# A seven-product second layer from group 1 on, and a planner that places batch 1's units

## The chip, the cores and the metric

The kernel runs on one core of a Trainium2 chip. A core has TensorE (PE) for matrix products, VectorE (DVE), ScalarE (ACT) and GpSimd (POOL) for elementwise work, and SyncE (SP), which here only issues DMAs. Each engine works through its own list of instructions in order, and semaphores tie the lists together. The metric is the time of one execution on the device in microseconds (us), as the median of several runs.

## The reference

The input x holds 8 batches of 3008 tokens with 256 channels. Each batch goes through a real Fourier transform along its tokens, is multiplied by a complex filter (1505 frequencies by 256 channels), and is transformed back. The result goes, token by token, through a feed-forward layer with a squared ReLU:

```python
X = np.fft.rfft(x, axis=1)
y = np.fft.irfft(X * (filt_r + 1j * filt_i)[None], n=3008, axis=1)
y = y.reshape(24064, 256)
h = np.maximum(y @ w_in, 0.0)          # w_in: 256 x 2048
out = (h * h) @ w_out                  # w_out: 2048 x 256
```

## The kernel before

**Feed-forward.** The 24064 tokens are cut into NG = 47 groups of 512, and each group into SLOTS = 8 slots. The main loop runs over all slots s, with g = s // 8 and k = s % 8. In a slot, `ffn_g1` computes an eighth of the first layer for group g (L553: four matmuls of 512 columns into psH, then the ReLU on ACT, L557); `ffn_sq` squares two slots' worth on DVE (L564). The second layer of a group runs one group later and takes one of two forms:

- the plain form, `ffn_g2` and `ffn_out`: eight matmuls of 256 columns a slot, 64 a group (L573), and two copies of psO by ACT (L584) before the stores;
- the seven-product form, for the groups in `SEVEN`: the product is split into a 2 x 2 block form, so that 7 block products of 16 matmuls with 128 columns each, 112 a group (L666), replace eight. `sums` makes four sums of the squared activations on DVE (L639, L642, L645, L648); `products` runs the matmuls one slot later than the plain form would, empties psX and psY by four copies on ACT and three additions on DVE (L681, L687), and stores in its sixth and seventh slot. `make_t` prepares four differences of the second layer's weights on DVE, once, in four slots.

In the kernel before, `SEVEN` is groups 6 to 45; groups 0 to 5 and 46 take the plain form. In the slot in which one form hands over to the other, no second-layer product runs.

**Fourier transform.** It is done by matmuls in small units, which run between the feed-forward's instructions. For batch b, 16 `unit_a` (L358) transform along one factor of the length and write u, which goes to DRAM (dU) and comes back turned round (`read_u`, ut). Then 12 `unit_b` (L442) each give a psB tile, from which DVE makes the product with the filter (L450); two DMAs on POOL's queue (L457) add its two halves. 12 `unit_p` (L487) do the first inverse step from that product; ACT copies psP to ze, and SP writes it to DRAM (dZ). `read_z` brings it back as zt, and 16 `unit_y` (L523) give the y that the feed-forward reads. Odd `unit_y` are copied out by DVE (L532), others by ACT (L530). `load_x` (L195, on POOL's queue) brings in the next batches. All four kinds of unit take their PSUM tile from one pool, psF, of two buffers.

**Order of work.** `fft_plan` writes a list of half slots. In a slot, the units of its first half come after `ffn_g1`, those of its second half after the second layer's products. Units in `fixed` go to the half slot that their formula gives, even where another is there already. Units in `units` are placed by a rule: each kind in turn, in the order `unit_b`, `unit_p`, `unit_y`, `unit_a`; each takes the free half slot nearest to its formula's, with a penalty where more than two of the four neighbours are taken. `moves` holds the DMAs, which may share a half slot. Batch 1's `unit_b` and `unit_p` are in `fixed`; those of later batches are in `units`. Batch 0 is transformed in a prologue before slot 0. A unit is written below as B1.4: `unit_b` number 4 of batch 1; A, P and Y likewise.

Of the kernel before, what the change touches and what calls it, by code (L numbers as in the profile page):

```python
# [20 lines left out]
SLOTS = 8  # L21
# [89 lines left out]
def kernel(  # L111
# [16 lines left out]
    NG = T // TG  # L128
# [408 lines left out]
    def ffn_g1(g, s):  # L537
        if s == 0:
            h2s[g] = p_h2.tile([128, NJT, TG], F16, tag="h2", name=f"h2_{g}")
        h2 = h2s[g]  # L540
        ps = psH(f"psH_{g}_{s}")
        segs = []
        t = g * TG
        while t < (g + 1) * TG:
            b, r = divmod(t, S)
            n = min((g + 1) * TG - t, S - r)
            segs.append((t - g * TG, b, r, n))
            t += n
        for i in range(2):
            jt = 2 * s + i  # L550
            for o, b, r, n in segs:
                for dt in range(2):
                    nc.tensor.matmul(ps[:, i, o:o + n],  # L553
                                     sWin[:, dt, jt * 128:(jt + 1) * 128],
                                     yts[b][:, dt, r:r + n],
                                     start=(dt == 0), stop=(dt == 1))
        nc.scalar.activation(out=h2[:, 2 * s:2 * s + 2, :], in_=ps, func=AF.Relu)  # L557
# [18 lines left out]
    def ffn_out(g, s):  # L576

        step = 1 if g == NG - 1 else 2
        if (s + 1) % (2 * step):
            return  # L580
        n = s // 2 + 1 - step
        ost = p_out.tile([128, 2, 256], F32, tag="ost", name=f"ost_{g}_{s}")
        h0 = n % 2
        nc.scalar.copy(out=ost[:, h0:h0 + step, :], in_=pso[g][:, h0:h0 + step, :])  # L584
        store(g, n, step, ost)
# [25 lines left out]
    def make_t(k):  # L611

        w = sWout.rearrange("p (q e) c -> p q e c", e=2)
        b11, b12 = w[:, :, 0, 0:128], w[:, :, 0, 128:256]
        b21, b22 = w[:, :, 1, 0:128], w[:, :, 1, 128:256]
        if k == 0:
            sg["t"] = p_t.tile([128, 4, 8, 128], F16, tag="t", name="sT")
        t = sg["t"]
        i0, i1 = ((b12, b11), (b22, t[:, 0]), (b22, b12), (b21, t[:, 1]))[k]
        nc.vector.tensor_sub(out=t[:, k], in0=i0, in1=i1)  # L620
        sg["w"] = {1: b11, 2: b21, 3: b22, 4: t[:, 3], 5: t[:, 0], 6: t[:, 1], 7: t[:, 2]}
# [33 lines left out]
    def products(g, k):  # L655

        f = sg[g]
        for p, m0, m1 in PARTS[k]:
            if p == 1 and m0 == 0:
                f["x"] = psO(f"psX_{g}").rearrange("p a (t c) -> p a t c", t=2)  # L660
            if p == 2 and m0 == 0:
                f["y"] = psO(f"psY_{g}").rearrange("p a (t c) -> p a t c", t=2)
            o = f["x"][:, 0] if p in (1, 6, 7, 4) else f["y"][:, 0 if p == 2 else 1]
            for m in range(m0, m1):
                q, t = divmod(m, 2)
                nc.tensor.matmul(o[:, t, :], f[p][:, q, 128 * t:128 * t + 128], sg["w"][p][:, q, :],  # L666
                                 start=(m == 0 and p in (1, 2)), stop=(q == 7),
                                 skip_group_check=True)
            if m1 < 16:
                continue  # L670
            if p == 1:
                f["top"] = p_out.tile([128, 2, 256], F32, tag="ost", name=f"top_{g}")
                nc.scalar.copy(out=f["top"][:, :, 0:128], in_=o)
            elif p == 6:
                nc.scalar.copy(out=f["top"][:, :, 128:256], in_=o)
            elif p == 7:
                f["bot"] = p_out.tile([128, 2, 256], F32, tag="ost", name=f"bot_{g}")
                nc.scalar.copy(out=f["bot"][:, :, 128:256], in_=o)
            elif p == 2:
                for v, i in ((f["top"][:, :, 0:128], 0), (f["bot"][:, :, 128:256], 1)):  # L680
                    nc.vector.tensor_add(out=v, in0=f["y"][:, i], in1=v)  # L681
            elif p == 4:
                nc.scalar.copy(out=f["bot"][:, :, 0:128], in_=o)
                store(g, 2, 2, f["bot"])
            elif p == 3:
                v = f["top"][:, :, 128:256]
                nc.vector.tensor_add(out=v, in0=o, in1=v)  # L687
                store(g, 0, 2, f["top"])
# [3 lines left out]
    def fft_plan():  # L692

        fixed, units, moves = [], [], []
        for b in range(1, B):
            f = (b * S // TG) * SLOTS - (48 if b > 1 else 40)
            d = 0
            if b == 1:
                for n in range(4, 16):
                    fixed.append(((n if n < 8 else n + 2 if n < 12 else 2 * n - 7) + n % 2 / 2,  # L700
                                  unit_y, 0, n))
                moves.append((7.5, read_z, 0, 3))
                for k in range(4):
                    moves.append(((4.5, 5.5, 7.5, 7.5)[k], cast_wout, k, nc.vector))
                for a in range(12, 16):
                    fixed.append((2 + a / 2, unit_a, b, a))
                moves.append((10.5, read_u, b))
                d = 7
            else:
                for a in range(16):  # L710
                    if a % 2 == 0 and b > 2:
                        moves.append((f + ((-57 + 2.3 * a) if b == 3 else (-66 + 2.75 * a)),
                                      load_x, b, a // 2))
                    units.append((f + (-16 + a, -46 + 2.1 * a, -56 + 2.75 * a)[min(b, 4) - 2],
                                  unit_a, b, a))
                moves.append((f + (2 if b == 2 else -6.5), read_u, b))
            for p in range(12):
                r = 14 + 15 * p / 11 if b == 1 else 6 + 28 * p / 11 if b == 2 else -2 + 36 * p / 11
                (fixed if b == 1 else units).append((f + r, unit_b, b, p))
                if b == 1 and 2 <= p < 10:  # L720
                    moves.append((f + r, load_x, 2, p - 2))
                (fixed if b == 1 else units).append((f + r + (4.5 if b == 1 else 7 - 2.5 * p / 11), unit_p, b, p))
            for c in range(4):
                moves.append((f + (40 + d / 7, 43, 48, 54)[c] - d, read_z, b, c))
            for n in range(16):
                (fixed if n < 4 else units).append((f + YN[n] - d, unit_y, b, n))
        work, used, done = {}, set(), {}
        for r, *u in fixed:
            h = int(2 * r)
            used.add(h)  # L730
            work.setdefault(h, []).append(u)
        rank = (unit_b, unit_p, unit_y, unit_a)
        for r, *u in sorted(units, key=lambda u: (rank.index(u[1]), u[0])):
            after = done.get((u[0], u[1]), -1)
            h = min((h for h in range(max(int(2 * r) - 3, after + 1), int(2 * r) + 12)
                     if h not in used),
                    key=lambda h: (sum(h + i in used for i in (-2, -1, 1, 2)) > 2) * 2
                    + abs(h - int(2 * r)))
            used.add(h)
            done[(u[0], u[1])] = h  # L740
            work.setdefault(h, []).append(u)
        for r, *u in moves:
            work.setdefault(int(2 * r), []).append(u)
        return work

    def run(plan, s, place):
        for f, *a in plan.get(2 * s + place, ()):
            f(*a)
# [10 lines left out]
    for k in range(2):  # L759
        c = slice(12 * k, 12 * k + 12)  # L760
# [26 lines left out]
    for k in range(6):  # L787
        if k % 3 == 0:
            sSPx.append(p_u.tile([128, 12, 128], F16, tag="u", name=f"sSPx_{k}"))
        c, o = slice(4 * k, 4 * k + 4), slice(4 * k % 12, 4 * k % 12 + 4)  # L790
# [26 lines left out]
    prologue[0] = False  # L817
    read_z(0, 2)

    SEVEN = range(6, NG - 1)  # L820
    work = fft_plan()

    for s in range((NG + 1) * SLOTS):
        g, k = divmod(s, SLOTS)
        if g < NG:
            ffn_g1(g, k)
        run(work, s, 0)
        if SEVEN[0] * SLOTS <= s < SEVEN[0] * SLOTS + 4:
            make_t(s % SLOTS)
        if (s - 1) // SLOTS - 1 in SEVEN:  # L830
            products((s - 1) // SLOTS - 1, (s - 1) % SLOTS)
        if g > 0 and g - 1 not in SEVEN:
            ffn_g2(g - 1, k)
        run(work, s, 1)
        if g > 0 and g - 1 not in SEVEN:
            ffn_out(g - 1, k)
        if g - 1 in SEVEN:
            sums(g - 1, k)
        if g < NG:
            ffn_sq(g, k)  # L840
# [30 lines left out]
```

## Time and profile before

| | before |
|---|---|
| median of 3 runs | 767.12 us (766.33 to 768.42) |
| the profiled execution's own time | 767.9 us |
| its span, first to last instruction | 766.1 us |
| PE busy | 751.9 us (98%) |
| DVE busy | 620.2 us (81%) |
| ACT busy | 579.2 us (76%) |
| POOL busy | 192.7 us (25%) |
| mean granted TensorE clock | 0.998 |

Busy times overlap: the engines work side by side. A matmul's end is modelled in the profile, and matmuls are pipelined, so that the time that one takes in a row of them is the distance between two starts and not the listed duration. Group 1 begins at 59.74 us, group 2 at 77.10, group 3 at 95.52, group 4 at 112.72, group 5 at 130.94, group 6 at 147.27 and group 7 at 163.82; each of these is the start of the group's first L553 matmul. Slot numbers count from slot 0, at 49.34 us.

### The profile page before, as it was taken

The numbers are of one execution on the slowest core, as the hardware profiler recorded it, in microseconds if no ns is written. First come the engines' busy times: TensorE is split into PE (matmuls) and PEld (weight loads), VectorE is DVE, ScalarE is ACT, GpSimd is POOL, SyncE is SP. The second block draws the span as 40 slices with busy tenths as digits, with TensorE's granted clock in tenths as the row PEclk, the third lists the DMA queues.
The fourth block names the chain that finished last, engine by engine and source line by source line (L and its number), as shares of the span: only waits on it lengthen the run. The fifth ranks groups of instructions, "written<-read, shape, count | busy, mean of one in ns | idle before, by whom it ended". The sixth has DMA issues, their size and how long they took to land.

```text
span 766.1 us, 19166 instructions
## 1 busy us (share of the span) xinstructions
PE 751.9 (98%) x8022; PEld 552.8 (72%) x8022; DVE 620.2 (81%) x679; ACT 579.2 (76%) x831; POOL 192.7 (25%) x260
## 2 busy tenths in 40 slices
PE   8989999999999999999999999999999999999998
PEld 6746666767777777877778777787777777777776
DVE  5856674579889888898979988798989989888783
ACT  3966777788878887788787877778876777777673
POOL 3800750133312331223212324043311222000000
PEclk9999999999999999999999999999999999999999
DMA  9985797756776457755575555765447334321011
GB/s 364 388 238 178 133 181 176 203 114 119 151 200 140 101 112 165 204 112 111 121 212 128 107 132 108 196 153 112 100 110 206 92 73 98 98 72 55 29 56 56
DMA packets 104943, 109.22 MB, mean 143 GB/s; under 512 B 9640, under 2 KB 93096, under 8 KB 102936
## 3 DMA queue, kind: packets, MB, share of 16 engines
q1 hardware_dynamic: 85704, 87.38, 36.8%
q0 software_dynamic: 19008, 20.43, 19.9%
q8 instruction: 63, 1.03, 0.6%
q14 instruction: 24, 0.20, 0.1%
q10 hardware_dynamic: 144, 0.18, 0.1%
HBM read 58.12 MB, written 48.23 MB: 139 GB/s over the span
## 4 chain that ended last, share of the span: by engine, by line
PE 87%; DVE 5%; DMA 5%; ACT 1%; issue 1%; SPq 0%; POOL 0%; DVEq 0%; ACTq 0%
PE psH L553 39%; PE psX L666 18%; PE psY L666 13%; PE psO L573 6%; PE psY L523 3%; PE psB L442 3%; PE psA L358 2%; DMA f<-in_filt_i_dram 2%; PE psP L487 2%; DVE prod L450 2%; DVE h L564 1%; DMA zt<-dZ 1%; DMA dZ<-ze 1%; PE psf L291 1%; DVE sum L645 1%
## 5 line engine op out<-in xcount | busy, mean ns | idle before, releaser
L557 ACT ACTIVATE h<-psH 128x1024 f16<-128x1024 f32 x376 | 385.0, 1025 | 153.3 <-PE psH L553 147.9
L553 PE MATMUL psH<-yt,sWin 128*128 128x512 f16 (+7 forms) x1728 | 388.5, 352 | 1.2 <-DVE yt L532 0.6
L564 DVE TENSOR_TENSOR h<-h 128x2048 f16<-128x2048 f16 (+1 forms) x192 | 229.9, 1198 | 55.2 <-ACT h L557 54.6
L457 POOL DMA_DIRECT2D prod<-prod x168 | 138.8, 970 | 440.1 <-DVE prod L450 432.8
L553 PEld LDWEIGHTS <-sWin 128*128 128x128 f16 x1728 | 152.8, 98 | 99.1 <-issue 5.0
L666 PEld LDWEIGHTS <-sum 128*128 128x128 f16 x2560 | 157.9, 98 | 18.4
L666 PEld LDWEIGHTS <-h 128*128 128x128 f16 x1920 | 118.9, 98 | 19.5
L450 DVE TENSOR_TENSOR prod<-psB,sF 128x1024 f16<-128x1024 f32 x84 | 102.5, 1220 | 25.2 <-PE psB L442 25.1
L666 PE MATMUL psX<-sT,sum 128*128 128x128 f16 x1280 | 91.0, 219 | 0.0
L666 PE MATMUL psY<-sT,sum 128*128 128x128 f16 x640 | 61.9, 219 | 0.0
L573 PE MATMUL psO<-sWout,h 128*128 128x256 f16 x448 | 56.9, 272 | 0.0
L532 DVE CAST yt<-psY 128x376 f16<-128x376 f32 x62 | 33.8, 545 | 27.5 <-PE psY L523 27.5
L362 ACT CAST u<-psA 96x512 f16<-96x512 f32 x90 | 52.1, 579 | 3.5 <-PE psA L358 3.1
L489 ACT CAST ze<-psP 128x512 f16<-128x512 f32 x84 | 49.0, 583 | 1.6 <-PE psP L487 1.6
L573 PEld LDWEIGHTS <-h 128*128 128x128 f16 x448 | 43.1, 98 | 9.1 <-issue 0.2
L642 DVE TENSOR_TENSOR sum<-sum,h 128x2048 f16<-128x2048 f16 x40 | 48.9, 1222 | 0.9
L666 PE MATMUL psY<-sWout,h 128*128 128x128 f16 x640 | 48.9, 219 | 0.0
L666 PE MATMUL psX<-sT,h 128*128 128x128 f16 x640 | 48.8, 219 | 0.0
L645 DVE TENSOR_TENSOR sum<-h 128x2048 f16<-128x2048 f16 x40 | 48.7, 1217 | 0.0
L648 DVE TENSOR_TENSOR sum<-h,sum 128x2048 f16<-128x2048 f16 x40 | 48.7, 1217 | 0.0
L666 PE MATMUL psY<-sWout,sum 128*128 128x128 f16 x640 | 48.6, 219 | 0.0
L639 DVE TENSOR_TENSOR sum<-h 128x2048 f16<-128x2048 f16 x40 | 48.6, 1216 | 0.0
(86 smaller groups left out, 684.4 us busy)
## 6 DMA issues: line engine op xcount, KB each, us to landing
zt<-dZ SPq DMA_DIRECT2D x64, 192.0 KB
dU<-u SPq DMA_DIRECT2D x28, 384.0 KB
prod<-prod POOLq DMA_DIRECT2D x168, 64.0 KB, 2.7
dZ<-ze SPq DMA_DIRECT2D x28, 384.0 KB
x<-in_x_dram POOLq DMA_DIRECT2D x40, 192.0 KB, 4.7
ut<-dU SPq DMA_DIRECT2D x7, 1024.0 KB
xw<-in_x_dram SPq DMA_DIRECT2D x6, 1024.0 KB
ut<-dU SPq DMA_DIRECT2D x7, 512.0 KB
```

The lines of the kernel that those rows point to most:

```text
L362: nc.scalar.copy(out=o, in_=pv)
L450: nc.vector.tensor_mul(out=prod, in0=ps.rearrange("p (a d) -> p a d", d=D).unsqueeze(1).to_broadcast([128, 2, 2, D]), in1=sF[:, :, 2 * p:2 ...
L457: nc.gpsimd.dma_start(out=prod[64 * i:64 * i + 64, 0], in_=prod[64 - 64 * i:128 - 64 * i, 1], accum_op=mybir.AluOpType.add)
L489: nc.scalar.copy(out=zes[(b, c)][:, 2 * i6:2 * i6 + 2, :], in_=ps.rearrange("p (a d) -> p a d", d=D))
L553: nc.tensor.matmul(ps[:, i, o:o + n], sWin[:, dt, jt * 128:(jt + 1) * 128], yts[b][:, dt, r:r + n], start=(dt == 0), stop=(dt == 1))
L557: nc.scalar.activation(out=h2[:, 2 * s:2 * s + 2, :], in_=ps, func=AF.Relu)
L564: nc.vector.tensor_mul(out=v, in0=v, in1=v)
L573: nc.tensor.matmul(pso[g][:, t % 2, :], h2s[g][:, jt, t * 128:(t + 1) * 128], sWout[:, jt, :], start=(jt == 0), stop=(jt == NJT - 1))
L642: nc.vector.tensor_sub(out=t, in0=f[5], in1=a11)
L645: nc.vector.tensor_sub(out=t, in0=a11, in1=a21)
L648: nc.vector.tensor_sub(out=t, in0=a12, in1=f[6])
L666: nc.tensor.matmul(o[:, t, :], f[p][:, q, 128 * t:128 * t + 128], sg["w"][p][:, q, :], start=(m == 0 and p in (1, 2)), stop=(q == 7), skip ...
```

## The change

The diff does three things.

- `SEVEN` starts at group 1 instead of group 6. `make_t` runs in slots 10 to 13 instead of 48 to 51. The slot without second-layer products is 16 instead of 56.
- Batch 1's `unit_b` and `unit_p` move from `fixed` to `units`, so that they are placed by the rule above, and their formula starts at 13.5 instead of 14. `load_x` of batch 2, which uses the same formula, moves by half a slot.
- The first `read_z` of batch 1 moves from half slot 34 to 33.5 (d is 7 for batch 1 and 0 for all others).

```diff
             for p in range(12):
-                r = 14 + 15 * p / 11 if b == 1 else 6 + 28 * p / 11 if b == 2 else -2 + 36 * p / 11
-                (fixed if b == 1 else units).append((f + r, unit_b, b, p))
+                r = 13.5 + 15 * p / 11 if b == 1 else 6 + 28 * p / 11 if b == 2 else -2 + 36 * p / 11
+                units.append((f + r, unit_b, b, p))
                 if b == 1 and 2 <= p < 10:
                     moves.append((f + r, load_x, 2, p - 2))
-                (fixed if b == 1 else units).append((f + r + (4.5 if b == 1 else 7 - 2.5 * p / 11), unit_p, b, p))
+                units.append((f + r + (4.5 if b == 1 else 7 - 2.5 * p / 11), unit_p, b, p))
             for c in range(4):
-                moves.append((f + (40 + d / 7, 43, 48, 54)[c] - d, read_z, b, c))
+                moves.append((f + (40 + d / 14, 43, 48, 54)[c] - d, read_z, b, c))
...
-    SEVEN = range(6, NG - 1)
+    SEVEN = range(1, NG - 1)
...
-        if SEVEN[0] * SLOTS <= s < SEVEN[0] * SLOTS + 4:
-            make_t(s % SLOTS)
+        if 10 <= s < 14:
+            make_t(s - 10)
```

## The prediction

> **What bounds the kernel now.** I read the busy times by group first. The stretches are cut at the first L553 matmul of groups 1 to 6, then a late group and the last whole one (us; busy us and instructions per engine; granted clock; DMA share; GB/s):
>
> ```profile
> 59.74:77.10 17.36, 16.91 (x124) 11.37 (x124) 10.71 (x14) 11.08 (x14) 0.59 (x2) 1.00 0.48 155
> 77.10:95.52 18.42, 17.45 (x136) 12.33 (x134) 11.37 (x10) 13.49 (x20) 13.79 (x19) 1.00 0.82 136
> 95.52:112.72 17.20, 17.20 (x122) 11.84 (x120) 11.75 (x11) 13.16 (x19) 10.93 (x15) 1.00 0.97 182
> 112.72:130.94 18.22, 17.31 (x127) 11.33 (x126) 8.79 (x10) 13.48 (x20) 1.01 (x2) 1.00 0.85 190
> 130.94:147.27 16.33, 16.14 (x158) 11.84 (x156) 8.19 (x9) 11.62 (x17) 0.79 (x2) 1.00 0.66 202
> 147.27:163.82 16.55, 16.55 (x128) 11.50 (x126) 11.71 (x14) 12.68 (x19) 6.92 (x10) 1.00 0.50 98
> 239.51:255.42 15.91, 15.76 (x175) 11.35 (x173) 14.75 (x16) 12.78 (x20) 4.71 (x7) 1.00 0.51 113
> 728.35:741.51 13.16, 13.16 (x148) 9.38 (x145) 10.46 (x11) 9.36 (x13) 0.00 (x0) 1.00 0.12 41
> ```
>
> TensorE sets the time: its columns fill the stretch but for 0.97 us in group 2 and 0.91 in group 4. DVE reaches 14.75 of 15.91 in a late seven-product group, and TensorE still hardly waits; groups 1 to 5 leave DVE 5.5 to 9.4 us.
>
> The chain of waits gives the price of both second products, and of one wait:
>
> ```profile
> 64.41 0.88 PE psO L573 x8
> ...
> 117.82 3.13 DMA dZ<-ze
> 121.02 6.49 DMA zt<-dZ
> ...
> 166.15 0.90 PE psX L666 x16
> ```
>
> Eight L573 matmuls take 0.88 us, 109 ns each; sixteen of L666 0.90, 56 ns each. The two DMAs are batch 1's inverse leaving and coming back; TensorE waits for them in slot 38. The waits of group 2, then of group 4, then DVE in order of time:
>
> ```profile
> PE psP L487 <- DVE prod L450: 0.6, 2, 0.3
> PE psB L442 <- ACT yt L530: 0.3, 1, 0.3
> ```
> ```profile
> PE psY L523 <- DMA zt<-dZ: 0.9, 1, 0.9
> ```
> ```profile
> 95.72 1.22 DVE L450 TENSOR_TENSOR prod<-psB,sF 128x1024 f16<-128x1024 f32 x1 [2.71 <-PE psB L442]
> 96.86 1.22 DVE L564 TENSOR_TENSOR h<-h 128x2048 f16<-128x2048 f16 x1
> 98.00 1.22 DVE L450 TENSOR_TENSOR prod<-psB,sF 128x1024 f16<-128x1024 f32 x1
> ```
>
> DVE starts its 1.22 us operations 1.14 us apart. By matmul starts (a modelled end hides part of a wait) group 2's three waits cost 0.51, 0.45 and 0.50 us, 1.46 in all: in half slots 19.5, 21 and 23.5 two or three units follow each other, and the last finds both psF banks full. Slot 38's costs 1.07.
>
> **The Trainium skill.** "TensorE: Matmul & The Clock Gate", Back-to-back issue gap, gives about 81 ns for a sustained 128-column matmul with its weights and 56 for an isolated one; the trace shows 56 sustained, so 56 counts. At 81, 112 matmuls would cost 9.07 us and the scheme would lose. "VectorE: DVE Perf Modes", the perf-mode tier table, has a 2-byte `tensor_tensor` of 2048 elements from SBUF at 1224 ns; the trace's sums take 1217 to 1222. "SBUF — State Buffer", Who interferes with whom: `tensor_tensor` does not starve GpSimd's descriptor writing. That agrees: one L457 takes 0.97 us on average, DVE at 81%, and 1.07 in groups 1 to 3, DVE at 65%. So the added sums should not slow POOL.
>
> **The change, part by part.** A slot is an eighth of a group. PE issue times: L553 4 x 216 ns = 0.864 per slot; unit_b or unit_p 2 x 109 = 0.218; unit_a 0.220; unit_y 4 x 41 = 0.165.
>
> 1. Second products of groups 1 to 5: 64 x 109 ns = 6.98 us becomes 112 x 56 = 6.27, so 0.70 each: **-3.52**. The slot without second products moves from 56 to 16; that changes no sum.
>
> 2. DVE gets four sums and three adds per group: 4 x 1.16 + 3 x 0.335 = 5.6 us. ACT gets four copies of 0.375 for two of 0.59, +0.3 on some 13 of 17: hidden under TensorE. make_t's four subtractions (0.68 each) go to slots 10 to 13, where group 1 leaves DVE 6.6 us; queued behind them are two psY evictions, at most 0.6 late, with the next taker of the bank a slot away; batch 1's last u cast (slot 9.5) is ahead. Cost 0.
>
> 3. The list gives each unit of batch 1 a half slot of its own. By its rule they are: B1.0 to B1.11 at 13, 14.5, 16, 17.5, 18.5, 20, 21.5, 23, 24, 25.5, 27, 28.5; P1.0 to P1.11 at 18, 19, 20.5, 22, 22.5, 25, 26.5, 28, 29, 30, 31.5, 33. A2.0 to A2.6 shift by up to 0.5; nothing else moves but batch 2's loads, which go with their unit_b. The triples of slots 19.5 and 23.5 are gone: **-1.46**.
>
> 4. B1.0 comes a full slot sooner, at 13. Its input was requested here:
>
> ```profile
> 69.76 0.82 SPq L433 DMA_DIRECT2D ut<-dU  x2
> ```
>
> By the packet records the first half's last 4 KB packet ends at 73.09 and its semaphore is complete at 73.45. B1.0 ran at 74.05 and did not wait; in slot 13 TensorE arrives at 71.28 + 0.86 = 72.15: **+1.30** (0.94 if the last packet counts). Nothing covers it, since TensorE runs in order; queued behind are group 0's second products and all that follows.
>
> 5. DVE in groups 2 and 3. Group 2: six products, four sums, four squares, two adds: 6 x 1.14 + 4 x 1.16 + 4 x 1.14 + 0.67 = 16.7 us. TensorE: 6.91 + 100 x 0.056 + 6 x 0.218 + 4 x 0.165 + 5 x 0.218 = 15.6. Group 3: 15.9 against 16.5; group 4: 14.2 against 16.3. DVE thus falls behind in slots 16 to 18 (three products, three sums, one square: 8.0 us against 5.3). Followed in program order with these times, B1.4's product ends 3.0 us after its matmuls begin instead of 1.3, so that in slot 19 the bank for Y0.13 comes 0.75 us late; then 0.06 in slot 22, 0.52 and 0.21 in slots 27 and 28, 0.12 in slot 52: **+1.66**. The bank is whichever comes free first: at 185.96 a psA matmul starts while DVE is still emptying the psB written two units before (185.78 to 187.00). If the two alternated strictly, the same working gives 3.5. Lower end 0.5: the same work in late groups costs only 0.3 in one group of six.
>
> 6. Products reach unit_p through POOL's accumulating DMAs. In the trace they land 3.4 to 7.5 us after the product, and unit_p still had 2.5 us or more in hand, except the last: landed 116.66, used 116.79. POOL needs 1.65 us for the pair and 1.15 for a load, 2.75 overlapped, against 1.36 slots x 2.07 = 2.8 between products: just enough. With the landing times of before, P1.4 has 0.2 us left and P1.11 lacks 0.5, the rest 0.9 or more: **+0.5** (0 to 1.9; the 97% DMA share speaks for more, the 256 KB store of slot 27 that now goes out in slot 31, behind it, for less).
>
> 7. read_z of batch 1 moves from 34 to 33.5, past A2.7's u write on SP. From P1.11 to slot 38 there are now 10.6 us (1.1 + 3 x 2.09 + 2.31 + 0.86). Before, write and read took 10.7 from P1.11, with the read's packets behind those of the u write. With the read ahead I take 8 to 9: **-1.07** (0 if it is no quicker and P1.11 is late as well). Stores of slots 31 and 32 wait for the adds and are issued before P1.11's copy is done.
>
> Sum: -3.52 - 1.46 + 1.30 + 1.66 + 0.50 - 1.07 = -2.59. The profiled span of 766.1 becomes 763.5. Its own time was 767.9, 1.8 over the span; the median of the runs is 767.12, so I forecast **764.5**.
>
> **Rivals.**
> - *DVE's lag costs nothing*: late groups run at 93% DVE (14.75 of 15.91) with 0.3 us of waits. Steps 5 and 6 vanish: -4.75, 762.4. Against it: unit_b comes every 1.4 slots here, every 2.5 to 3.3 in later batches.
> - *DVE becomes the bound of groups 2 and 3*: banks alternate and P1.11 is 1.7 late: +1.8 and +1.2 on the forecast, so +0.4 against before, 767.5. For it: 16.7 us of DVE work against 15.6 of TensorE.
> - *Slower*: the accumulates of batch 1. POOL's cover is 2% and the DMA share 97%; if the last accumulate lands later, TensorE waits in slot 33 by the excess. At 10.1 us after its product (7.5 before) the gain is gone; from 12.4 on the kernel is slower by 0.3%; at 13 it takes 770.0. For it: landing time grew from 4.0 to 7.5 us through group 3. Against: the store that leaves the queue ahead of it.
>
> **How the numbers follow.** 0.3%, 2.3 us, is about what a measurement can tell from no change; the forecast, -2.6, lies near that edge. Forecast case 0.58, its own range 763.3 to 766.3 (step 5 from 0.5 to 3.5): faster in 0.34, within in 0.24. No lag: 0.17, faster. DVE bound: 0.17, of which 0.15 within and 0.02 slower. Late accumulates: 0.08, of which 0.03 within and 0.05 slower. Faster 0.51, within 0.42, slower 0.07. Range 762.2 to 767.5: it leaves out part of the no-lag case and the slower ends.
>
> **What would show it.** Group 5, with no product of batch 1: 0.7 shorter, 15.6 us. A wait for `ut` of about 1.3 us at B1.0 in slot 13. In group 2, psP and psB waits for DVE gone at 19.5 and 23.5, new short ones in slots 19 to 22 and 27 to 28. Groups 2, 3, 4 at about 16.5, 17.2 and 16.9 us. No wait for `zt` in slot 38, or a short one. The forecast is wrong if slot 13 shows no wait, if group 2 lasts over 17.5 us, or if unit_p waits in slots 22 to 33 by more than 1 us.

## The result, and the profile after

The changed kernel takes 764.12 us (763.39 to 765.42, six runs) beside 767.03 us for the kernel before in the same comparison: a ratio of 0.9962, with a 95% interval from 0.9946 to 0.9979. The forecast was 764.5 us, within 762.2 to 767.5. The profiled span went from 766.1 to 763.6 us; the forecast of it was 763.5.

Busy times of the changed kernel by group, cut as before, at the first L553 matmul of groups 1 to 7 (us; busy us and instructions of PE, PEld (TensorE's weight loads), DVE, ACT and POOL; granted clock; DMA share; GB/s):

```profile
60.10:79.11 19.01, 17.09 (x125) 11.30 (x124) 13.89 (x18) 10.86 (x14) 1.69 (x2) 1.00 0.48 147
79.11:95.43 16.32, 15.73 (x173) 11.58 (x171) 15.95 (x17) 13.28 (x21) 12.36 (x17) 1.00 0.78 120
95.43:112.62 17.19, 16.95 (x174) 11.96 (x172) 16.57 (x18) 13.36 (x21) 11.15 (x16) 1.00 0.95 177
112.62:128.91 16.29, 16.29 (x175) 11.32 (x172) 14.06 (x17) 13.54 (x22) 1.01 (x2) 1.00 0.97 228
128.91:144.76 15.85, 15.67 (x206) 11.86 (x204) 13.62 (x16) 12.17 (x19) 0.63 (x2) 1.00 0.66 209
144.76:160.60 15.84, 15.84 (x178) 11.52 (x175) 14.65 (x16) 12.45 (x20) 6.84 (x10) 1.00 0.53 101
```

Group 1 grew from 17.36 to 19.01 us, group 2 shrank from 18.42 to 16.32, group 3 hardly moved, group 4 shrank from 18.22 to 16.29. DVE now works 15.95 of 16.32 us in group 2 and 16.57 of 17.19 in group 3, where it had 11.4 and 11.8 before. The waits show what moved. Below are three lines of those from 69 to 98 us (waiting engine and line, what released it; us in total, times, longest), and then the request for the input of B1.0, in the view of SP in order of time:

```profile
PEld L442 <- DMA ut<-dU: 1.8, 1, 1.8
...
PE psB L442 <- DMA ut<-dU: 1.3, 1, 1.3
...
PE psY L523 <- ACT ze L489: 0.6, 1, 0.6
```

```profile
70.26 0.82 SPq L433 DMA_DIRECT2D ut<-dU  x2
```

The waits of psP and psB of group 2 before are gone, a wait for `ut` in slot 13 is new, and so is one in slot 19. The wait for `zt` in slot 38 is gone: no such line is left from 95 to 131 us.

Spans differ by up to 2.5 us before slot 8 from one execution to another, whatever the kernel, and slot 8 itself lasts from 3.10 to 3.37 us (last section). So the experiments are read from the distance between the first matmuls of slot 8 and slot 64, which holds the whole change, and beside it from slot 9 on, where that spread is left out; after slot 64 all kernels take the same time within 0.4 us. The distance from slot 8 is 119.37 us before and 116.41 after: -2.96. From slot 9 it is 116.16 and 113.04: -3.12.

| kernel | slots 8 to 64, us | slots 9 to 64, us | ratio to the kernel before | 95% interval |
|---|---|---|---|---|
| before | 119.37 | 116.16 | 1 | |
| changed | 116.41 | 113.04 | 0.9962 | 0.9946 to 0.9979 |
| seven_only | 119.23 | 115.86 | 1.0001 | 0.9990 to 1.0011 |
| place_only | 117.92 | 114.80 | 0.9987 | 0.9979 to 0.9995 |
| no_sums | 114.89 | 111.52 | 0.9940 | 0.9924 to 0.9955 |
| ut_split | 114.91 | 111.54 | 0.9943 | 0.9926 to 0.9961 |
| u_on_act | 116.60 | 113.49 | 0.9972 | 0.9964 to 0.9979 |
| b_at_14 | 116.05 | 112.94 | 0.9962 | 0.9947 to 0.9976 |
| z_at_34 | 116.77 | 113.66 | one run | |
| split_act | 114.99 | 111.88 | 0.9951 | 0.9934 to 0.9967 |
| split_a1 | 114.08 | 110.97 | 0.9931 | 0.9917 to 0.9944 |
| after_again | 116.09 | 112.98 | 0.9963 | 0.9950 to 0.9975 |

### The profile page after: what moved, and what is told of

Read it like the earlier page. It is cut to its first block, busy times and chain, and to the rows that moved or that the text cites. A ratio compares the mean times of both kernels' runs of the same rounds, so it can differ in the third digit from the quotient of the medians.

```text
span 763.6 us, 19701 instructions
## 1 busy us (share of the span) xinstructions
PE 749.8 (98%) x8262; PEld 552.9 (72%) x8262; DVE 645.8 (85%) x714; ACT 578.8 (76%) x841; POOL 192.4 (25%) x260
## 4 chain that ended last, share of the span: by engine, by line
PE 88%; DVE 6%; DMA 3%; ACT 1%; issue 1%; POOL 0%; SPq 0%; ACTq 0%; DVEq 0%
PE psH L553 39%; PE psX L666 20%; PE psY L666 14%; PE psB L442 3%; PE psY L523 2%; PE psA L358 2%; PE psP L487 2%; DVE h L564 2%; PE psO L573 2%; DVE prod L450 1%; DMA ut<-dU 1%; PE warm L272 1%; DMA dU<-u 1%; PE psf L291 1%; PE psf L294 1%
## 5 line engine op out<-in xcount | busy, mean ns | idle before, releaser
L553 PE MATMUL psH<-yt,sWin 128*128 128x512 f16 (+7 forms) x1728 | 388.3, 352 | 1.4 <-DVE yt L532 0.6
L457 POOL DMA_DIRECT2D prod<-prod x168 | 138.6, 965 | 438.0 <-DVE prod L450 429.1
L553 PEld LDWEIGHTS <-sWin 128*128 128x128 f16 x1728 | 152.2, 98 | 99.4 <-issue 4.8
L666 PEld LDWEIGHTS <-sum 128*128 128x128 f16 x2880 | 177.5, 98 | 20.2 <-issue 0.2
L666 PEld LDWEIGHTS <-h 128*128 128x128 f16 x2160 | 133.6, 98 | 21.0
L450 DVE TENSOR_TENSOR prod<-psB,sF 128x1024 f16<-128x1024 f32 x84 | 102.4, 1219 | 16.4 <-PE psB L442 16.2
L666 PE MATMUL psX<-sT,sum 128*128 128x128 f16 x1440 | 102.5, 219 | 0.0
L666 PE MATMUL psY<-sT,sum 128*128 128x128 f16 x720 | 69.7, 219 | 0.0
L642 DVE TENSOR_TENSOR sum<-sum,h 128x2048 f16<-128x2048 f16 x45 | 55.0, 1222 | 1.0
L666 PE MATMUL psY<-sWout,h 128*128 128x128 f16 x720 | 55.0, 219 | 0.0
L666 PE MATMUL psX<-sT,h 128*128 128x128 f16 x720 | 54.9, 219 | 0.0
L645 DVE TENSOR_TENSOR sum<-h 128x2048 f16<-128x2048 f16 x45 | 54.8, 1217 | 0.0
L639 DVE TENSOR_TENSOR sum<-h 128x2048 f16<-128x2048 f16 x45 | 54.7, 1215 | 0.0
L666 PE MATMUL psX<-sWout,h 128*128 128x128 f16 x720 | 47.6, 219 | 0.0
L523 PEld LDWEIGHTS <-zt 112*128 112x128 f16 x512 | 33.5, 98 | 18.5 <-issue 4.3
```

The source lines that it names most:

```text
L450: nc.vector.tensor_mul(out=prod, in0=ps.rearrange("p (a d) -> p a d", d=D).unsqueeze(1).to_broadcast([128, 2, 2, D]), in1=sF[:, :, 2 * p:2 ...
L457: nc.gpsimd.dma_start(out=prod[64 * i:64 * i + 64, 0], in_=prod[64 - 64 * i:128 - 64 * i, 1], accum_op=mybir.AluOpType.add)
L553: nc.tensor.matmul(ps[:, i, o:o + n], sWin[:, dt, jt * 128:(jt + 1) * 128], yts[b][:, dt, r:r + n], start=(dt == 0), stop=(dt == 1))
L639: nc.vector.tensor_add(out=t, in0=a21, in1=a22)
L642: nc.vector.tensor_sub(out=t, in0=f[5], in1=a11)
L645: nc.vector.tensor_sub(out=t, in0=a11, in1=a21)
```

## The experiments

**seven_only: the seven products without the new placement.** The kernel before with `SEVEN` from group 1 on and `make_t` in slots 10 to 13; batch 1's units and its read_z as before.

```diff
-    SEVEN = range(6, NG - 1)
+    SEVEN = range(1, NG - 1)
...
-        if SEVEN[0] * SLOTS <= s < SEVEN[0] * SLOTS + 4:
-            make_t(s % SLOTS)
+        if 10 <= s < 14:
+            make_t(s - 10)
```

> Groups 1 to 5 take the seven-product form; batch 1's units and its read_z stay where they were. My theory (DVE falls behind, and the psF banks that it empties late stop TensorE where units share a half slot): the 3.5 us of matmul time are nearly all given back. Group 2 about 18.3 us (before 18.42), group 3 about 18.3 (before 17.20), waits of 0.5 to 0.9 us in slots 19, 21 and 23 and three or four of 0.1 to 0.75 in slots 25 to 29; no wait for ut at B1.0; the wait for zt in slot 38 stays at about 1 us. The kernel is 0 to 0.7 us shorter than before. Rival, the parts add up: the second products are worth 0.7 us a group wherever the units are, so the kernel is 3.5 us shorter than before, groups 2 and 3 at 17.7 and 16.5.

Measured: ratio 1.0001, slots 8 to 64 shorter by 0.14 us, slots 9 to 64 by 0.30. Groups 2 and 3 took this (busy times as above):

```profile
77.20:95.51 18.31, 16.22 (x172) 11.68 (x170) 16.20 (x16) 14.17 (x23) 13.73 (x19) 1.00 0.77 120
95.51:113.66 18.15, 17.07 (x170) 11.96 (x168) 17.02 (x18) 12.91 (x20) 10.67 (x16) 1.00 0.94 175
```

In group 2 (slots 16 to 23) and in groups 3 and 4, TensorE waited for this:

```profile
PE psB L442 <- ACT yt L530: 0.7, 1, 0.7
PE psP L487 <- ACT yt L530: 0.6, 1, 0.6
PE psY L523 <- DVE prod L450: 0.5, 1, 0.5
PE psP L487 <- DVE prod L450: 0.4, 1, 0.4
```

```profile
PE psY L523 <- DMA zt<-dZ: 1.2, 1, 1.2
PE psB L442 <- ACT u L362: 0.6, 1, 0.6
PE psB L442 <- DVE u L364: 0.3, 1, 0.3
PE psA L358 <- DVE prod L450: 0.3, 1, 0.3
```

By its place, each of these lines but that of `zt` is a unit that finds both psF banks full. The units stand where they stood before, but DVE has 16.2 and 17.0 us of work instead of 11.4 and 11.8, and what it should have emptied is late. So nearly all of the 3.5 us of matmul time came back as waits. The parts do not add up.

**place_only: the new placement without the seven products.** The changed kernel with the last two edits of the diff above undone.

```diff
-    SEVEN = range(1, NG - 1)
+    SEVEN = range(6, NG - 1)
...
-        if 10 <= s < 14:
-            make_t(s - 10)
+        if SEVEN[0] * SLOTS <= s < SEVEN[0] * SLOTS + 4:
+            make_t(s % SLOTS)
```

> Groups 1 to 5 keep the plain form; batch 1's units are placed by the list from 13.5 on and read_z goes to 33.5. My theory: the wait for ut in slot 13 costs 1.3 to 1.5 us in full (group 1 at 18.7), the three waits of group 2 are gone (16.95), group 3 stays at 17.2, and the wait of slot 38 is gone (group 4 at 17.0): 1.0 to 1.3 us shorter than before. If the store of slot 27 is what delays the last accumulate, unit_p 11 waits here for 0.5 us or more in slot 33, which it did not in the changed kernel. Rival, the parts add up: the whole change is worth 2.9 us and the second products 3.5, so that this kernel is 0.6 us longer than before.

Measured: slots 8 to 64 shorter by 1.45 us, slots 9 to 64 by 1.36, ratio 0.9987. Groups 1 to 4:

```profile
58.02:76.59 18.57, 17.08 (x124) 11.30 (x124) 11.23 (x14) 10.86 (x14) 1.70 (x2) 1.00 0.56 167
76.59:93.57 16.98, 16.98 (x136) 12.21 (x134) 11.50 (x10) 13.03 (x19) 12.60 (x17) 1.00 0.82 136
93.57:110.78 17.21, 17.21 (x126) 11.90 (x124) 11.06 (x12) 13.19 (x19) 10.91 (x15) 1.00 0.98 179
110.78:127.77 16.99, 16.99 (x126) 11.36 (x124) 8.83 (x10) 13.46 (x20) 1.01 (x2) 1.00 0.87 212
```

TensorE is busy for the whole of groups 2 to 4. The three waits of group 2 and the one of slot 38 are gone, and slot 13 is 1.53 us longer: 1.30 of wait for `ut`, and B1.0 itself. Slot 33 is 0.15 us shorter as well. So P1.11 had waited there in the kernel before, by 0.15 us: its accumulate landed 0.13 us ahead of it, and where P1.11 plainly waits (u_on_act, below) that distance is 0.14. The last accumulate landed 1.6 us before P1.11, 6.1 us after its product, although the store of slot 27 goes out ahead of it in this kernel. So that store alone is not what made it land so late before: that guess of mine falls. Alone, the two parts bring 0.14 and 1.45 us; together they bring 2.96 (from slot 9: 0.30, 1.36 and 3.12). The other 1.4 us exist only where the list spreads the units that a busy DVE must serve.

**no_sums: DVE's added work taken away.** The changed kernel; for groups 1 and 2 the four sums are left out, and the block products read one of a sum's inputs instead. The matmuls are the same in number and shape.

```diff
+        if g in (1, 2):
+            sg[g].update({5: a21, 6: a11, 7: a11, 3: a12})
+            return
```

> The changed kernel without the four sums of groups 1 and 2 (they would run on DVE in slots 16 to 20 and 24 to 28): the block products take one of the sum's inputs in its place, so these two groups' outputs are not the reference's. The matmuls are the same. My theory, DVE's lag is the 1.5 us of group 2 and 3 over TensorE's own 15.57 and 16.46: group 2 about 15.6, group 3 about 16.5, no waits in slots 19 to 28, the kernel 1.4 to 1.6 us shorter than the changed one. Rival, the waits come from the placement itself or from POOL's accumulates: groups 2 and 3 stay at 16.3 and 17.2.

Measured: groups 2 and 3 fall to TensorE's own time:

```profile
78.58:94.16 15.58, 15.58 (x173) 11.55 (x171) 11.95 (x13) 13.20 (x21) 12.64 (x17) 1.00 0.83 135
94.16:110.69 16.53, 16.53 (x173) 11.85 (x171) 12.20 (x14) 13.14 (x21) 10.93 (x16) 1.00 0.99 182
```

The prediction's sums for TensorE were 15.6 and 16.5. So 0.74 us of group 2 and 0.66 of group 3 in the changed kernel are due to the sums on DVE. That includes the wait of slot 19, which the profile puts down to ACT (`ACT ze`): the unit takes the bank that ACT empties, because the other is still with DVE.

**ut_split: a smaller first piece for B1.0.** The changed kernel with batch 1's `read_u` in three pieces; the first holds the 2 columns that B1.0 reads.

```diff
-        for s0, s1 in ((0, 8), (8, 24)):
+        for s0, s1 in ((0, 2), (2, 8), (8, 24)) if b == 1 else ((0, 8), (8, 24)):
```

> The changed kernel with batch 1's read_u in three pieces, of 2, 6 and 16 of the 24 columns, instead of 8 and 16, so that the piece that B1.0 needs is 128 KB instead of 512. My theory, the wait of slot 13 costs its whole length: that wait falls from 1.47 us to 0.5 or less, and the kernel is 1.0 to 1.5 us shorter than the changed one; groups 2 and 3 as there, give or take 0.2. Rival, the wait is absorbed (DVE and POOL use it to get ahead, so that the waits of slots 19 to 28 grow by as much without it): no shorter than the changed kernel by more than 0.3.

Measured: 1.50 us shorter than the changed kernel, ratio 0.9943. Group 1 takes 17.52 us and the wait of slot 13 is wholly gone; group 2 is what it was:

```profile
59.66:77.18 17.52, 16.91 (x125) 11.38 (x124) 13.88 (x18) 10.86 (x14) 1.69 (x2) 1.00 0.53 159
77.18:93.50 16.32, 15.73 (x173) 11.58 (x171) 15.95 (x17) 13.29 (x21) 12.37 (x17) 1.00 0.79 121
```

The wait cost its full length; nothing was absorbed.

**u_on_act: part of DVE's work moved to ACT.** All u casts of batch 2 on ACT.

```diff
-        if a % 2 == 0 or b > 2:
+        if a % 2 == 0 or b > 1:
```

> The changed kernel with all u casts of batch 2 on ACT; its odd ones (0.61 us each, slots 26 to 40) leave DVE. ACT's share in groups 3 and 4 rises by about 2 us, to 15 of 17. My theory, DVE's lag makes the 0.73 us of group 3 over TensorE's own 16.46: group 3 at 16.5 to 16.8, group 2 unchanged at 16.3, group 4 at 16.3, the kernel 0.4 to 0.7 us shorter than the changed one. Rival, group 3 waits for POOL's accumulates (P1.5 had only 1.3 us in hand): group 3 stays at 17.2. Second rival, ACT becomes the late one: waits for the ReLU of psH, groups 3 and 4 longer than 17.2 and 16.3.

Measured: group 3 fell to 16.61 us, as DVE's lag demands, but group 4 rose from 16.29 to 17.33, and the kernel gained nothing: from slot 9 on it takes 0.45 us more than the changed kernel (ratio to the kernel before 0.9972). ACT, with 14.2 of 16.6 and 15.8 of 17.3 us, is not the late one. The waits of groups 3 and 4 name another:

```profile
PE psP L487 <- DMA prod<-prod: 0.9, 1, 0.9
```

P1.11 waits for its accumulate, which landed 7.6 us after the product (115.73 after 108.13); in the changed kernel it landed after 5.7 us (114.25 after 108.58), 0.98 us before it was needed. This is the mechanism of the prediction's sixth step and of its slower rival, in a kernel that was meant to be faster. The view of SP in order of time shows what else moved. This kernel, then the changed one:

```profile
109.49 0.33 SPq L341 DMA_DIRECT2D dU<-u  x1
```

```profile
110.34 0.33 SPq L341 DMA_DIRECT2D dU<-u  x1
```

With A2.3's cast on ACT the first u write of batch 2 (384 KB) leaves SP 1.4 us after the last product instead of 1.8.

**b_at_14: half a slot later again.** The changed kernel with batch 1's formula at 14, still placed by the list.

```diff
-                r = 13.5 + 15 * p / 11 if b == 1 else 6 + 28 * p / 11 if b == 2 else -2 + 36 * p / 11
+                r = 14 + 15 * p / 11 if b == 1 else 6 + 28 * p / 11 if b == 2 else -2 + 36 * p / 11
```

> The changed kernel with batch 1's units from 14 on instead of 13.5, still placed by the list: B1.0 at 14, B1.11 at 29, P1.11 at 33.5. My theory: no wait for ut (group 1 at 17.5 instead of 19.0), group 2 at 16.2, group 3 0.5 us longer at 17.7, slot 38 waits for zt again by 0.3 to 1.1 us since P1.11 comes half a slot later: between 0.8 us shorter than the changed kernel and 0.3 longer. Rival, the half slot is what brought the gain: 1 us or more longer than the changed kernel.

Measured: slots 8 to 64 shorter than in the changed kernel by 0.36 us, of which 0.26 lie in slot 8 and 0.10 behind it, with the same ratio, 0.9962. The `ut` wait of slot 13 is gone (group 1: 17.26 us); groups 2 and 3 are 16.58 and 17.55, with other waits for DVE's banks. I expected a wait for `zt` in slot 38; there is none. Instead slots 27 and 46 wait. The first line is P1.6 in slot 27, the second B2.0 in slot 46:

```profile
PE psP L487 <- DVE prod L450: 0.9, 1, 0.9
PE psB L442 <- DMA ut<-dU: 0.7, 1, 0.7
```

The list now finds 40.5 taken and puts A2.15 at 42, where batch 2's read_u is also due, so batch 2's last u write leaves SP only 3.2 us before that read (132.79 and 136.03), and B2.0 waits. The half slot itself was worth nothing: it trades one wait for another.

**z_at_34: the inverse read back behind the u write.** The changed kernel with `d / 7`.

```diff
-                moves.append((f + (40 + d / 14, 43, 48, 54)[c] - d, read_z, b, c))
+                moves.append((f + (40 + d / 7, 43, 48, 54)[c] - d, read_z, b, c))
```

> The changed kernel with batch 1's first read_z back at 34, behind A2.7's write of u on SP; P1.11 stays at 33. In the changed kernel the write of dZ took 4.9 us and the read 3.2, and slot 38 had about half a microsecond to spare. My theory, being ahead of the u write is what keeps the read short: the read lands later by 1 us or more and TensorE waits in slot 38 for 0.4 to 1.2 us (group 4 at 16.7 to 17.5). Rival, P1.11's half slot alone removed the wait: no wait in slot 38, group 4 at 16.3.

Measured: group 4 takes 17.01 us instead of 16.29, all of it in slot 38. Its waits, and the chain of waits there:

```profile
PE psY L523 <- DMA zt<-dZ: 0.6, 1, 0.6
```

```profile
115.04 4.81 DMA dZ<-ze
119.91 4.68 DMA zt<-dZ
```

The write takes 4.8 us and the read 4.7. In the changed kernel, with the read ahead of the u write, the write was issued at 116.96 and complete at 122.25, and the read, issued at 122.31, was complete by 125.45: 3.1 us. From the write's issue to the read's end that is 9.55 us here and 8.49 there. The same distance is 9.5 to 9.7 us in the three kernels with the read behind the u write (before, seven_only and this one) and 7.7 to 8.7 in the nine with it ahead. The place on SP's queue is worth 0.72 us of slot 38. How the time is shared between write and read is not settled by the place: in place_only the read is ahead too and takes 5.5 us, after a write of 3.1.

**split_act: both edits of ut_split and u_on_act.**

> The changed kernel with both edits that aim at its waits: batch 1's read_u in pieces of 2, 6 and 16 columns, and the u casts of batch 2 on ACT. If the waits are separate, the gains add: 1.9 to 2.1 us shorter than the changed kernel (group 1 at 17.5, 2 at 16.3, 3 at 16.6, 4 at 16.3). If they share a cause, it is no better than the one with the split read alone (1.5 us).

Measured: slots 8 to 64 take 114.99 us, 0.08 more than with the split read alone; from slot 9 on it is 0.34 more. Group 3 took 16.61 us and group 4 17.20, with P1.11 waiting again (0.8 us for `prod`). By my expectation's wording this would mean that both waits share a cause. They don't: the second edit brings its 0.58 us in group 3, and a new wait in group 4 takes more than that back.

**split_a1: only the cast that is late.** The split read, and of batch 2's casts only that of A2.1 on ACT.

```diff
-        if a % 2 == 0 or b > 2:
+        if a % 2 == 0 or b > 2 or (b, a) == (2, 1):
```

> The changed kernel with the split read_u, and of batch 2's u casts only that of A2.1 (slot 26) moved to ACT; A2.3's stays on DVE, so that the first u write of batch 2 leaves SP no sooner than in the changed kernel, behind the last accumulate. My theory: A2.1's cast is what makes the bank late in slot 27, and in the kernels with all casts on ACT it was the earlier u write that made the accumulate for P1.11 land 7.6 us after its product. So group 3 is at 16.7 to 16.9, unit_p 11 waits by less than 0.3 us in slot 33, and the kernel is 1.8 to 2.0 us shorter than the changed one. Rival, the accumulate lands late because TensorE gets there sooner and the DMA engines are full, whoever writes: a wait of 0.5 to 1.1 us in slot 33 and a gain of 1.0 to 1.4 us.

Measured: 761.65 us, ratio 0.9931 (0.9917 to 0.9944), slots 8 to 64 at 114.08: 2.33 us less than in the changed kernel's first profile, of which 0.26 lie in slot 8, and 2.01 less than in its second (after_again, below). This beats both kernels. Groups 1 to 4:

```profile
58.43:75.69 17.26, 16.91 (x124) 11.38 (x124) 13.62 (x18) 10.86 (x14) 1.69 (x2) 1.00 0.64 187
75.69:92.01 16.32, 15.73 (x173) 11.58 (x170) 15.95 (x17) 13.29 (x21) 12.36 (x17) 1.00 0.81 122
92.01:108.62 16.61, 16.60 (x173) 11.87 (x171) 15.97 (x17) 13.74 (x22) 11.16 (x16) 1.00 0.97 184
108.62:124.91 16.29, 16.29 (x174) 11.32 (x172) 14.06 (x17) 13.55 (x22) 1.01 (x2) 1.00 0.95 229
```

Group 3 has the whole gain of u_on_act and group 4 none of its loss. P1.11 does not wait: its accumulate landed 6.1 us after the product, 0.61 us before it was needed, and the u write left 1.8 us after the product, as in the changed kernel. TensorE reaches slot 33 as early relative to the product as in u_on_act, and the DMA share in group 3 is nearly as high (0.97 against 1.00), so TensorE's early arrival alone does not make the accumulate late. That the u write's earlier start does is what these runs point to, but it is not shown: the write was not moved by itself, and seven_only does not fit a simple rule. There the u write left SP 2.2 us before the product's end, and the accumulate landed after 5.0 us, the shortest time of all; in the kernel before it left 1.7 us before that end, and the accumulate landed after 7.5.

**after_again: the changed kernel beside it.**

> The changed kernel itself, timed beside the one above. Both theories: slots 8 to 64 take 116.4 us as before, 0.995 to 0.998 of the kernel before in time.

Measured: 763.66 us, ratio 0.9963, slots 8 to 64 at 116.09. Slot 13 is 0.05 us shorter than in the first profile and slot 8 0.26 us; every group from 2 on is the same within 0.01 us.

## Why the prediction was right, step by step

1. *Second products, -3.52.* Right: group 6 fell by 0.72 us, as 64 x 109 ns against 112 x 56 say. Group 5 fell by only 0.48; the prediction had 0.7. The rest is in slot 47 of the changed kernel. There DVE does B2.0's product first (142.61 to 143.83) and then the two additions that empty psY, and the block product that writes psY again begins 0.25 us late, when the second of them ends at 144.49. Both, in order of time:

```profile
144.08 0.41 DVE L681 TENSOR_TENSOR bot<-psY,bot 128x256 f32<-128x256 f32 x1
144.54 0.38 PE L666 MATMUL psY<-sWout,sum 128*128 128x128 f16 x4
```

This is DVE's lag again, by another buffer than the fifth step had in view.

2. *DVE's and ACT's other added work in group 1, 0.* Right: in seven_only slots 10 to 13, with make_t in them, are as long as before.
3. *The shared half slots, -1.46.* Right: place_only's group 2 fell by 1.44.
4. *The wait for `ut`, +1.30.* Right in kind; it measured 1.48, because the input was complete 3.83 us after its request (at 74.09) instead of 3.69, and the matmul began 0.05 us after that. The request, at 70.26 instead of 69.76, was no later beside TensorE's own work: 6.79 us after the start of slot 9, 6.81 before. ut_split gives all of the wait back.
5. *DVE's lag, +1.66.* Measured 0.75 in group 2 and 0.73 in group 3, 1.48 in all, of which no_sums removes 1.40. The place was right as well: slot 19 for group 2 and slots 27 and 28 for group 3. Against no_sums these two are longer by 0.36 and 0.19 us (forecast 0.52 and 0.21), and slot 25, which was not forecast, by 0.10.
6. *The accumulates, +0.5.* Wrong in size: no wait in the changed kernel. The prediction carried over the 7.5 us that the last accumulate had taken; it took 5.7. Its reason for a shorter time, the store of slot 27, explains little of that (place_only has the store ahead of the accumulate and took 6.1). u_on_act shows the mechanism with the time that was feared: 7.6 us, and 0.9 us of wait. That the added sums would not slow POOL holds, though the prediction set a mean (0.97 us for one L457) beside a median (1.07): by the mean, one L457 of groups 1 to 3 takes 0.99 us before and 0.97 after, while DVE's share there rises from 64% to 88%.
7. *read_z, -1.07.* Right in sum, but for less comfortable a reason. The prediction took 8 to 9 us for write and read; from P1.11 at 115.23 to the read's end at 125.45 they took 10.2, with 0.6 to spare. The write was issued 1.7 us after P1.11 began instead of 1.0, since slot 33's ReLU is now ahead of the copy on ACT. The read's second half fell from 6.5 to 3.1 us, as argued, but the write before it rose from 3.1 us to 5.3 (116.96 to 122.25). The six pieces of two stores (512 KB) now leave SP in the 3.5 us ahead of it; the write took 3.1 us in both kernels with one store there (before, place_only) and 3.4 to 5.3 in those with two. No run moved the stores alone. The step names them but gives them no cost.

The measured terms, -3.52 - 1.44 + 1.48 + 1.48 - 1.07, give -3.07; with the 0.25 us of slot 47 and the 0.15 of slot 33 that the prediction had not counted as a wait, -2.97. From slot 9 on, -3.12 were measured, so about 0.15 us stay unassigned. The predicted sum, -2.59, was 0.5 too small. That is the size of step 6; the other errors (0.18 too little in step 4 and too much in step 5, slots 33 and 47) about cancel, which is luck. The profiled span hides the difference: slot 8 came 0.36 us later in the changed kernel's execution and was 0.16 us longer, and 763.5 against 763.6 is closer than the working deserves. Of the signs that the prediction named, two came out otherwise: group 4 at 16.29 us instead of 16.9 (step 6) and group 5 at 15.85 instead of 15.6 (slot 47). None of its signs of being wrong came.

Of the rivals, "DVE's lag costs nothing" falls by no_sums, and "DVE becomes the bound of groups 2 and 3" describes not this kernel but seven_only, where those groups take 18.3 and 18.2 us. The slower rival's mechanism is real, but in the changed kernel the last accumulate lands 0.98 us ahead, of which some 0.84 are room.

## What to carry to other kernels

When an edit saves time on the engine that sets the pace and adds work to a neighbour, look for the buffers that the neighbour empties. Here 3.5 us of saved matmul time were worth 0.1 to 0.3 us until the units that share two PSUM banks were spread out. Starting a unit sooner is only worth as much as its input is early, and a smaller first piece of the input can be cheaper than a later start. After each wait removed, ask which transfer had been hidden behind it: casts moved to a less busy engine freed 0.58 us and sent a write off 0.4 us sooner, next to an accumulate that had less than 1 us to spare.

## What was not expected of the hardware

- The landing of one and the same DMA depends on what surrounds it by more than the room that a schedule leaves. The last accumulate of batch 1 (two halves of 64 KB) landed 7.5 us after its product in the kernel before, and 5.0 to 7.6 in the experiments; the write of dZ took from 3.1 to 5.3 us, the second half of the read of zt from 3.1 to 6.5.
- The first matmuls of slot 0 run at two speeds from one execution to another, whatever the kernel. In the profile of the kernel before they start 0.43 us apart until 52.6 us, in that of place_only 0.21, and the granted clock of the same stretch shows it; both views by stretch, the kernel before first:

```profile
49.30:53.00 3.70, 3.66 (x9) 1.26 (x9) 0.35 (x1) 1.19 (x2) 0.00 (x0) 0.57 1.06 260
```

```profile
49.30:53.00 3.70, 3.40 (x15) 1.36 (x15) 0.92 (x1) 2.70 (x3) 0.00 (x0) 1.00 1.06 273
```

In the kernel before, the trace has TensorE at full clock from 5.42 us on, at half from 49.79 to 53.20 us, which is 3.41 us, and then at full again. The Trainium skill ("TensorE: Matmul & The Clock Gate", What's actually happening) has a window of about 3.4 us that does not start with the kernel, and half the clock after an idle one. The length agrees. But the 3.41 us ahead were not idle: TensorE paused in them for 1.05 us (46.84 to 47.89), with matmuls on both sides, and place_only, with a pause of 0.99 us (46.41 to 47.40), kept its full clock. What decides between the two is not shown. With the lower clock group 0 lasts 10.40 us instead of 9.17. That is 1.2 us of span with nothing changed, four tenths of what this change is worth. Slot 8 differs too: one and the same kernel, the changed one, took 3.37 us for it in the profile with the lower clock and 3.11 in the one without, though u_on_act took 3.11 with it. Hence the distances from slots 8 and 9 on.
